# The chunk of the last 64 rows first, the weights' integer steps through a PSUM bank, the weights' conversions spread evenly

## The chip, the cores and the metric

The kernel runs on one core of a Trainium2 chip. A core has five engines that run side by side, each through its own list of instructions in order: PE (TensorE, matrix multiplies; its weight loads are shown as PEld), DVE (VectorE), ACT (ScalarE), POOL (GpSimd) and SP (SyncE, which here only issues DMA transfers). The metric is the device time of one execution in microseconds (us). Before the change it is 705.91 us, the median of three runs (705.66 to 707.59).

## The reference

An attention layer with a learned position bias feeds a two-matrix feed-forward layer. All arrays are float32.

```python
B, H, S, D = 4, 8, 576, 64            # batch, heads, rows, head width
scores = (1/sqrt(D)) * q @ k.T
rel = pos[:, None] - pos[None, :]
x = log1p(abs(rel)) / log1p(max(pos[:, None], 1))
bias = relu(x[..., None] @ w1 + b1) @ w2          # hidden 32, one column per head
attn = softmax(scores + bias per head)
x = (attn @ v) as 2304 rows of 512                # 2304 = B*S, 512 = H*D
h = relu(x @ w_in)                                # w_in 512 x 2048
out = (h*h) @ w_out                               # w_out 2048 x 512
```

## The kernel before

**Work by steps.** Batches are taken in pairs p = 0, 1. The 576 rows of a batch are cut into five chunks c: c = 1 to 4 are 128 rows each, and c = 0 is the last 64 rows. In a whole chunk the two batches of the pair lie side by side (nb = 2 blocks of 128 rows); in c = 0 the 64 rows of both batches share one block (nb = 1). A step is one (p, c, head): 10 chunks of 8 heads, 80 steps, counted here from 0. `ORDER` gives the order of the chunks, for pair 0 `[3, 0, 2, 4, 1]`. So steps 0 to 7 are chunk 3, steps 8 to 15 the half chunk 0, steps 16 to 23 chunk 2.

**A step.** `qk` writes the scores to PSUM (three fp16 products of split operands), `softmax_a` adds the bias and takes the maximum on DVE (line 367, one instruction for each block, with a small read of the maximum and the negation of line 370 behind it) and the exponential on ACT (line 373). `softmax_b` splits the result into two fp16 parts on ACT and POOL (lines 118, 384, 385), and a DMA transposes it. `pv` multiplies by v three steps later (`LAG`), and after a chunk's last head `finish_x` scales the chunk's rows, splits and transposes them.

**The bias.** The bias depends on the row and on the distance alone, so it is made once, in 36 groups of 16 rows, and written to a table in DRAM (`biasd`), from which each step reads its window (`bias_ld`, tile bt). `hgen` makes four hidden layers of a group (tile hg), each on DVE (line 266) or on ACT (line 263) as the digit of `HID` says (the digit is how many of the four go to ACT, one digit for two groups in their order of use); `bias_mm` multiplies them on PE (line 293), copies the result out on ACT or DVE (line 304) and stores it. A chunk's groups must be in DRAM before its first step; `bias_due` says how many groups are made by which step, `AHEAD` = 3 steps in advance.

**The weights.** w_in and w_out come in 32 loads of 512 KB (`WT`, called W below), through three staging buffers (stg) that k and v use too. Each is turned from float32, passed in as 64-bit words, into two fp16 parts. Three integer steps on DVE put the word's halves together (lines 185, 186, 188; tile cv in SBUF, which is input and output of the second and third), then ACT or POOL make the high part and POOL the low one (line 203). `W_AT` lists how many W are put behind k and v at each step.

**The feed-forward part.** A finished chunk becomes 8 units. A unit's `g1` is 24 matmuls into hp (line 465), then a ReLU on ACT, the square on DVE (line 473) and a split; `g2` (line 488) adds into one output bank for each block: o0, and for a whole chunk o1 as well. o0 and o1 have one PSUM bank each. A unit is started about once a step, and g2 runs three units behind g1 (`GLAG`). Units of a half chunk are half the width.

**The order.** The program is written step by step, and a scheduler of the tile framework then orders the instructions of each engine with its own estimates; the lists are fixed before the kernel runs.

Of the kernel before, what the change touches and what calls it, by code (L numbers as in the profile page):

```python
# [8 lines left out]
F32 = mybir.dt.float32  # L9
F16 = mybir.dt.float16  # L10
U32 = mybir.dt.uint32
# [5 lines left out]
B, H, S, D = 4, 8, 576, 64  # L17
# [15 lines left out]
    "ev": "AAAADD", "er": "AAAADA", "gh": "PPPPDD",  # L33
}

HID = "110033320111212000"

W_AT = [0, 0, 0, 0, 2, 0, 0, 0, 0, 2, 3, 0, 5, 0, 3, 4, 0, 4, 1, 0, 2, 1, 0, 2, 0, 0, 1, 0, 1, 0, 1, 0]
ORDER = [[3, 0, 2, 4, 1], [1, 0, 4, 2, 3]]
LAG, GLAG = 3, 3  # L40
BACKLOG = 10
AHEAD = 3
# [4 lines left out]
def tile_attention_moe(  # L47
# [11 lines left out]
    nc = tc.nc  # L59
    PS = bass.MemoryType.PSUM  # L60

    def pool(name, bufs, **kw):
        return ctx.enter_context(tc.tile_pool(name=name, bufs=bufs, **kw))
# [24 lines left out]
    ps_o = pool("ps_o", 1, space=PS)  # L88
# [75 lines left out]
    class WT:  # L164
# [14 lines left out]
        def split(self):  # L179
            u, q = self.u, self.part  # L180
            wd = self.st.bitcast(U32).rearrange("p (n t) -> p n t", t=2)
            lo32, hi32 = wd[:, :, 0], wd[:, :, 1]
            cv = r_p.tile([128, 512], F32, tag="r", name="cv")
            ci = cv.bitcast(U32)
            nc.vector.tensor_scalar(ci, hi32, 3, 0x3FFFFFFF, op0=ALU.logical_shift_left, op1=ALU.bitwise_and)  # L185
            nc.vector.scalar_tensor_tensor(out=ci, in0=lo32, scalar=29, in1=ci,  # L186
                                           op0=ALU.logical_shift_right, op1=ALU.bitwise_or)
            nc.vector.scalar_tensor_tensor(out=ci, in0=hi32, scalar=0xC0000000, in1=ci,  # L188
                                           op0=ALU.bitwise_and, op1=ALU.bitwise_or)
            if self.which == "i":  # L190
                st = cv.rearrange("p (k f) -> p k f", k=2)
                f0 = slice(u * 256, (u + 1) * 256)
                hi, lo, e = winH[:, 2 * q:2 * q + 2, f0], winL[:, 2 * q:2 * q + 2, f0], WIS
            else:
                st = cv
                hi, lo, e = woutH[:, u * 2 + q, :], woutL[:, u * 2 + q, :], WOS
            cast(zn("wh", u), hi, st, float(2 ** e))
            if zn("wl", u) == "D":
                nc.vector.scalar_tensor_tensor(
                    out=lo, in0=st, scalar=float(2 ** e), in1=hi, op0=ALU.mult, op1=ALU.subtract)  # L200
            else:
                cast(zn("wl", u), st, st, float(2 ** e))
                nc.gpsimd.tensor_tensor(lo, st, hi, op=ALU.subtract)  # L203
# [300 lines left out]

    order = [(p, c) for p in range(2) for c in ORDER[p]]
    steps = [(p, c, h) for p, c in order for h in range(H)]
    NS = len(steps)
    groups, due = [], []
# [2 lines left out]
        due.append(len(groups))  # L511

    def bias_due(t):
        k = (t + AHEAD) // H + 1
        if k >= NCK:
            return len(groups)
        f = (t + AHEAD) % H + 1
        return due[k - 1] + -(-(due[k] - due[k - 1]) * f // H)

    loads = deque()  # L520
# [5 lines left out]
    nls = []  # L526
    w_at = W_AT
    for h in range(H):
# [186 lines left out]
```

## Time and profile before

| what | value |
|---|---|
| median of three runs | 705.91 us |
| the profiled execution | 710.13 us |
| its span on the core | 708.4 us |
| PE busy | 611.1 us (86%) |
| DVE busy | 453.9 us (64%) |
| ACT busy | 357.3 us (50%) |
| POOL busy | 385.4 us (54%) |

The trace is of the profiled execution, so sums are made against its 710.13 us, of which 1.7 us lie outside the span. A profile row of an engine gives its busy share in 40 slices of the span; the shares over the whole span are averages over a first part and a second part that look quite different, so most rows below are of stretches of the span. "PEclk" is the granted clock of TensorE as a share of its full speed.

### The profile page before, as it was taken

How to read it: one execution, taken by the hardware profiler on the slowest of the kernel's cores; microseconds unless marked ns; L12 is line 12 of the kernel's file. 1: busy time of each engine (PE TensorE's matmuls, PEld its weight loads, DVE VectorE, ACT ScalarE, POOL GpSimd, SP SyncE). 2: the span in 40 equal slices, each digit the busy share in tenths (PEclk: the TensorE clock that was granted, in tenths of full speed). 3: DMA queues.
4: the chain of work that ended last, by engine and by line, in shares of the span. 5: the costliest groups of instructions: out<-in, count | busy, mean ns of one | idle time of the engine just before them, and what ended most of it. 6: DMA issues, size and time to landing. Idle time of an engine off the chain costs nothing.

```text
span 708.4 us, 15644 instructions
## 1 busy us (share of the span) xinstructions
PE 611.1 (86%) x6056; PEld 377.9 (53%) x6056; DVE 453.9 (64%) x977; ACT 357.3 (50%) x710; POOL 385.4 (54%) x375
## 2 busy tenths in 40 slices
PE   6635535687797998999998999999998999999997
PEld 1112213454454544666665667666665666676764
DVE  8687999699995687468757645335557656334120
ACT  5778645655676653654553453244464664531111
POOL 4266665568695544676676554435555566442211
PEclk9858557899797999999999999999999999999999
DMA  7699999997795898797896978375799978461000
GB/s 217 213 239 279 225 235 259 233 258 196 194 240 143 175 227 165 158 185 162 211 237 128 174 168 150 84 143 114 141 153 205 190 156 155 95 131 31 25 7 30
DMA packets 235881, 119.25 MB, mean 168 GB/s; under 512 B 196384, under 2 KB 212768, under 8 KB 235808
## 3 DMA queue, kind: packets, MB, share of 16 engines
q1 hardware_dynamic: 235808, 118.27, 74.1%
q8 instruction: 47, 0.77, 0.4%
q14 instruction: 26, 0.21, 0.1%
HBM read 55.44 MB, written 15.61 MB: 100 GB/s over the span
## 4 chain that ended last, share of the span: by engine, by line
PE 52%; DVE 18%; DMA 14%; issue 6%; ACT 5%; POOL 4%; SPq 0%; DVEq 0%; POOLq 0%; ACTq 0%
PE hp L465 20%; PE o L488 19%; DMA at<-a 7%; PE pv L411 5%; PE sc L352 3%; PE bp L293 3%; DVE hg L266 3%; DVE cv L186 3%; POOL a L385 2%; DVE s L367 2%; DVE cv L188 2%; DVE cv L185 2%; DMA biasd<-be 1%; ACT s L373 1%; ACT a L118 1%
## 5 line engine op out<-in xcount | busy, mean ns | idle before, releaser
L465 PE MATMUL hp<-xt,winH 128*128 128x256 f16 (+1 forms) x1280 | 202.4, 268 | 15.3 <-DVE r L473 14.0
L488 PE MATMUL o<-woutH,g 128*128 128x512 f16 x576 | 184.4, 380 | 0.9 <-ACT o L495 0.9
L373 ACT ACTIVATE s<-s,nm 128x576 f32<-128x576 f32 x144 | 110.5, 768 | 136.6 <-DVE nm L370 136.1
L465 PE MATMUL hp<-xt,winL 128*128 128x256 f16 (+1 forms) x640 | 165.7, 267 | 0.3 <-POOL winL L203 0.3
L385 POOL TENSOR_TENSOR a<-s,a 128x1024 f16<-128x1024 f32 (+1 forms) x80 | 162.6, 2033 | 0.0
L465 PEld LDWEIGHTS <-winH 128*128 128x128 f16 x1280 | 118.7, 100 | 51.3 <-issue 20.1
L367 DVE CUSTOM_DVE_ANT_0 s<-sc,bt 128x576 f32<-128x576 f32 x144 | 103.4, 750 | 45.3 <-PE sc L352 23.3
L488 PEld LDWEIGHTS <-g 128*128 128x128 f16 x864 | 82.8, 98 | 90.4 <-issue 6.7
L473 DVE TENSOR_TENSOR r<-hp,r 128x512 f32<-128x512 f32 (+1 forms) x80 | 50.6, 633 | 117.0 <-ACT r L471 116.6
L475 POOL TENSOR_TENSOR g<-r,g 128x512 f16<-128x512 f32 (+1 forms) x80 | 86.8, 1085 | 66.8 <-DVE g L122 64.4
L411 PEld LDWEIGHTS <-at 128*128 128x128 f16 (+1 forms) x2240 | 80.6, 105 | 71.3 <-DMA at<-a 38.7
L384 POOL TENSOR_TENSOR a<-s,a 128x128 f16<-128x128 f32 (+1 forms) x80 | 37.0, 463 | 146.5 <-ACT a L118 118.5
L411 PE MATMUL pv<-v,at 128*128 128x64 f16 (+1 forms) x2240 | 88.8, 199 | 30.7 <-DMA at<-a 28.9
L118 ACT ACTIVATE a<-s 128x1152 f16<-128x1152 f32 (+1 forms) x80 | 85.1, 1064 | 49.9 <-DMA at<-a 48.9
L488 PE MATMUL o<-woutL,g 128*128 128x512 f16 x288 | 109.4, 380 | 0.0
L471 ACT ACTIVATE r<-hp 128x512 f32<-128x512 f32 (+1 forms) x80 | 43.2, 540 | 64.9 <-PE hp L465 64.3
L266 DVE TENSOR_SCALAR hg<-tab_t,nb 128x352 f32<-128x352 f32 (+17 forms) x102 | 67.1, 708 | 13.1 <-PE bp L293 11.4
L293 PE MATMUL bp<-hg,w2s 128*32 128x288 f32 (+17 forms) x352 | 62.0, 550 | 14.8 <-ACT be L304 10.4
L465 PEld LDWEIGHTS <-winL 128*128 128x128 f16 x640 | 64.0, 100 | 8.2 <-issue 0.8
L352 PE MATMUL sc<-k,q 64*128 64x512 f16 x384 | 57.0, 398 | 0.0
L304 ACT ACTIVATE be<-bp,hcst 128x288 f32<-128x288 f32 (+32 forms) x80 | 34.5, 473 | 20.8 <-PE bp L293 14.4
L122 DVE TENSOR_SCALAR g<-r 128x512 f16<-128x512 f32 (+1 forms) x61 | 40.0, 656 | 2.1
(61 smaller groups left out, 551.4 us busy)
## 6 DMA issues: line engine op xcount, KB each, us to landing
bt<-biasd SPq DMA_DIRECT2D x64, 288.0 KB, 3.3
stg<-w_in SPq DMA_DIRECT2D x16, 512.0 KB, 4.3
stg<-w_out SPq DMA_DIRECT2D x16, 512.0 KB, 4.2
stg<-vd SPq DMA_DIRECT2D x16, 320.0 KB, 3.8
stg<-kd SPq DMA_DIRECT2D x16, 288.0 KB, 3.8
bt<-biasd SPq DMA_DIRECT2D x32, 144.0 KB, 3.5
qst<-qd SPq DMA_DIRECT2D x32, 128.0 KB, 3.5
out<-o SPq DMA_DIRECT2D x16, 256.0 KB, 2.4
```

The lines of the kernel that those rows point to most:

```text
L118: nc.scalar.activation(out=out, in_=in_, func=AF.Copy, scale=scale)
L266: nc.vector.tensor_scalar(ht, tab_t[:, 0:dlen(G)], scl[:, n:n + 1], nb1, op0=ALU.mult, op1=ALU.max)
L293: nc.tensor.matmul(out=bp[32 * t:32 * t + 32, 0:d1 - d0], lhsT=w2s, rhs=ts_[t][:, d0:d1], start=True, stop=True, tile_position=(0, 32 * t))
L352: nc.tensor.matmul(out=sc[:, 1024 * b:1024 * b + 512], lhsT=qt[r, qz, qs], rhs=kt[r, z, 64 * b:64 * b + 512], start=(n == 0), stop=(n == 2 ...
L367: nc.vector.tensor_tensor_reduce(s[:, 576 * b:576 * b + 576], sc[:, 960 * b:960 * b + 576], bt, inv, -3.0e38, ALU.add, ALU.max, mx[:, b:b ...
L373: nc.scalar.activation(out=sl, in_=sl, func=AF.Exp, bias=nm[:, b:b + 1], accum_out=su[:, h, b:b + 1])
L385: nc.gpsimd.tensor_tensor(av[:, :, 640:1152], ev[:, :, 0:512], av[:, :, 0:512], op=ALU.subtract)
L411: nc.tensor.matmul(out=dst, lhsT=lhsT, rhs=vt[:, vz, 5 * b + blk, :], start=(n == 0), stop=(n == 13), tile_position=(0, 0 if c else 64 * b))
L465: nc.tensor.matmul(out=hp[:, f * T:f * T + T].rearrange("p (b t) -> p b t", b=nb), lhsT=wt[:, k, c0:c0 + 128], rhs=xt[:, 0:nb, z * 4 + k, ...
L473: nc.vector.tensor_tensor(rr, hp[:, 0:2 * T], rr, op=ALU.mult)
L475: nc.gpsimd.tensor_tensor(g[:, 1, 0:2 * T], r[:, 0:2 * T], g[:, 0, 0:2 * T], op=ALU.subtract)
L488: nc.tensor.matmul(out=blk["o"][b], lhsT=g[:, z, c0:c0 + 128], rhs=wt[:, 2 * u + f, :], start=(u == 0 and f == 0 and z == 0 and wt is wout ...
```

## The change

Four things are changed together. The half chunk c = 0 of pair 0 becomes the first chunk (steps 0 to 7) and chunk 3 the second. The first two of the three integer steps of a W write to a tile `ci` in the PSUM bank of o1, and the third reads it from there and writes cv in SBUF. `W_AT` puts all 32 W into steps 0 to 15. `HID` is another table, and `bias_due` asks for the first chunk's groups alone before step 0 and looks ahead less in the first steps.

```diff
-HID = "110033320111212000"
+HID = "333222111111111000"
-W_AT = [0, 0, 0, 0, 2, 0, 0, 0, 0, 2, 3, 0, 5, 0, 3, 4, 0, 4, 1, 0, 2, 1, 0, 2, 0, 0, 1, 0, 1, 0, 1, 0]
-ORDER = [[3, 0, 2, 4, 1], [1, 0, 4, 2, 3]]
+W_AT = [1, 1, 2, 2, 2, 2, 2, 2, 3, 3, 3, 2, 2, 2, 2, 1] + [0] * 16
+ORDER = [[0, 3, 2, 4, 1], [1, 0, 4, 2, 3]]
...
             cv = r_p.tile([128, 512], F32, tag="r", name="cv")
-            ci = cv.bitcast(U32)
+            ci = ps_o.tile([128, 512], F32, tag="o1", name="ci").bitcast(U32)
             nc.vector.tensor_scalar(ci, hi32, 3, 0x3FFFFFFF, op0=ALU.logical_shift_left, op1=ALU.bitwise_and)
             nc.vector.scalar_tensor_tensor(out=ci, in0=lo32, scalar=29, in1=ci,
                                            op0=ALU.logical_shift_right, op1=ALU.bitwise_or)
-            nc.vector.scalar_tensor_tensor(out=ci, in0=hi32, scalar=0xC0000000, in1=ci,
+            nc.vector.scalar_tensor_tensor(out=cv.bitcast(U32), in0=hi32, scalar=0xC0000000, in1=ci,
                                            op0=ALU.bitwise_and, op1=ALU.bitwise_or)
...
     def bias_due(t):
-        k = (t + AHEAD) // H + 1
+        if t < 0:
+            return due[0]
+        ahead = min(AHEAD, t + 1)
+        k = (t + ahead) // H + 1
         if k >= NCK:
             return len(groups)
-        f = (t + AHEAD) % H + 1
+        f = (t + ahead) % H + 1
```

In the lists of the changed kernel the line numbers from 185 on are one higher. DVE just ahead of step 0 (the first line with ISA s,mx), before:

```order
L266 TENSOR_SCALAR hg<-tab_t,nb_131 128x528
L157 SCALAR_TENSOR_TENSOR v<-stg,v 128x640
L266 TENSOR_SCALAR hg<-tab_t,nb_131 128x544
L146 SCALAR_TENSOR_TENSOR k<-stg,k 128x576
L157 SCALAR_TENSOR_TENSOR v<-stg,v 128x640
L266 TENSOR_SCALAR hg<-tab_t,nb_131 128x560
L146 SCALAR_TENSOR_TENSOR k<-stg,k 128x576
L367 ISA s,mx<-sc,bt 128x576
```

The same place now:

```order
L189 SCALAR_TENSOR_TENSOR cv<-stg,ci 128x512
L157 SCALAR_TENSOR_TENSOR v<-stg,v 128x640
L186 TENSOR_SCALAR ci<-stg 128x512
L187 SCALAR_TENSOR_TENSOR ci<-stg,ci 128x512
L267 TENSOR_SCALAR hg<-tab_t,nb_131 128x304 x3
L189 SCALAR_TENSOR_TENSOR cv<-stg,ci 128x512
L267 TENSOR_SCALAR hg<-tab_t,nb_131 128x320 x2
L186 TENSOR_SCALAR ci<-stg 128x512
L187 SCALAR_TENSOR_TENSOR ci<-stg,ci 128x512
L368 ISA s,mx<-sc,bt 128x576
```

Ahead of step 0 stand 31 hg and no W before, and 10 hg and two whole W now. The second place is DVE ahead of step 16, the first of chunk 2 (r is the square of a feed-forward unit). Before:

```order
L186 SCALAR_TENSOR_TENSOR cv<-stg,cv 128x512
L188 SCALAR_TENSOR_TENSOR cv<-stg,cv 128x512
L266 TENSOR_SCALAR hg<-tab_t,nb_131 128x336
L473 TENSOR_TENSOR r<-hp,r 128x512
L266 TENSOR_SCALAR hg<-tab_t,nb_131 128x336 x2
L367 ISA s,mx<-sc,bt 128x576
```

And now (r is half as wide, and the hg are already those of chunk 4):

```order
L474 TENSOR_TENSOR r<-hp,r 128x256
L186 TENSOR_SCALAR ci<-stg 128x512
L187 SCALAR_TENSOR_TENSOR ci<-stg,ci 128x512
L189 SCALAR_TENSOR_TENSOR cv<-stg,ci 128x512
L186 TENSOR_SCALAR ci<-stg 128x512
L267 TENSOR_SCALAR hg<-tab_t,nb_131 128x416 x3
L187 SCALAR_TENSOR_TENSOR ci<-stg,ci 128x512
L424 TENSOR_TENSOR x<-pv,rd 128x256 x2
L368 ISA s,mx<-sc,bt 128x576
```

Of the 32 W, 11 stood behind step 16; now 2 do. Counted in the lists, this is what stands ahead of a step's first line 367 on DVE and first score matmul on PE (hp and o in matmuls):

| ahead of step | W | hg on DVE | r | bias matmuls | hp | o |
|---|---|---|---|---|---|---|
| 0, before / now | 0 / 2 | 31 / 10 | 0 / 0 | 11 / 8 | 0 / 0 | 0 / 0 |
| 8 | 7 / 12 | 38 / 30 | 0 / 0 | 76 / 76 | 0 / 0 | 0 / 0 |
| 16 | 21 / 30 | 58 / 48 | 3 / 2 | 100 / 88 | 72 / 24 | 24 / 0 |
| 24 | 32 / 32 | 76 / 69 | 10 / 10 | 132 / 128 | 240 / 216 | 96 / 48 |
| 32 | 32 / 32 | 102 / 96 | 19 / 19 | 176 / 176 | 456 / 456 | 144 / 144 |

The third place is ACT at the start of the program, where the hidden layers (hg), the copies of the bias (be) and k's corner (kz) stand. Before:

```order
L263 ACTIVATE hg<-tab_t,sm_t 128x320
L263 ACTIVATE hg<-tab_t,sm_t 128x304 x2
L263 ACTIVATE hg<-tab_t,sm_t 128x320
L304 ACTIVATE be<-bp,hcst 128x320
L304 ACTIVATE be<-bp,hcst 128x271
L151 ACTIVATE kz<-k 64x2x64 x2
L304 ACTIVATE be<-bp,hcst 128x304
```

And now:

```order
L264 ACTIVATE hg<-tab_t,sm_t 128x528 x3
L264 ACTIVATE hg<-tab_t,sm_t 128x544 x3
L264 ACTIVATE hg<-tab_t,sm_t 128x560 x3
L264 ACTIVATE hg<-tab_t,sm_t 128x576 x3
L151 ACTIVATE kz<-k 64x2x64 x2
L264 ACTIVATE hg<-tab_t,sm_t 128x320 x2
L305 ACTIVATE be<-bp,hcst 128x64
```

Twelve hidden layers of the half chunk's four groups now stand ahead of the first copy.

## Rows read from the trace of the kernel before

**Rows 1.** The page: the span, and the 40 slices of PE (tenths of a slice busy).

```profile
span 708.4 us, 15644 instructions
...
PE   6635535687797998999998999999998999999997
```

**Rows 2.** Where steps 0, 8, 16, 24 and 32 begin: the first line 367 of each in DVE's timeline (start us, us).

```profile
32.40 0.76 DVE L367 CUSTOM_DVE_ANT_0 s<-sc,bt 128x576 f32<-128x576 f32 x1
...
90.94 0.74 DVE L367 CUSTOM_DVE_ANT_0 s<-sc,bt 128x576 f32<-128x576 f32 x1
...
159.68 0.75 DVE L367 CUSTOM_DVE_ANT_0 s<-sc,bt 128x576 f32<-128x576 f32 x1
...
235.56 0.76 DVE L367 CUSTOM_DVE_ANT_0 s<-sc,bt 128x576 f32<-128x576 f32 x1 [1.45 <-DMA bt<-biasd]
...
301.07 0.76 DVE L367 CUSTOM_DVE_ANT_0 s<-sc,bt 128x576 f32<-128x576 f32 x1
```

**Rows 3.** The stretches between those steps: window, length, then busy us (instructions) of PE, PEld, DVE, ACT, POOL, granted clock, share of the DMA engines, GB/s.

```profile
32.00:91.00 59.00, 27.80 (x277) 12.61 (x277) 50.32 (x94) 43.56 (x87) 37.39 (x34) 0.67 0.95 252
91.00:160.00 69.00, 42.56 (x424) 25.51 (x424) 60.91 (x106) 38.68 (x78) 42.75 (x42) 0.78 1.01 245
160.00:236.00 76.00, 63.28 (x590) 34.82 (x588) 65.69 (x118) 47.74 (x94) 55.06 (x48) 0.87 0.80 192
236.00:301.00 65.00, 60.81 (x640) 33.41 (x637) 44.11 (x102) 36.35 (x77) 33.56 (x34) 1.00 0.85 183
301.00:361.00 60.00, 58.62 (x602) 39.42 (x600) 43.21 (x93) 32.45 (x70) 41.34 (x46) 1.00 0.85 191
```

**Rows 4.** The same for the instructions that touch cv alone; the first pair is DVE.

```profile
32.00:91.00 59.00, 21.16 (x23) 7.70 (x13) 7.79 (x6) 0.67 0.95 252
91.00:160.00 69.00, 31.87 (x43) 15.14 (x26) 20.78 (x18) 0.78 1.01 245
160.00:236.00 76.00, 33.45 (x31) 11.20 (x19) 19.83 (x16) 0.87 0.80 192
```

**Rows 5.** Shortest, median and longest duration in ns of the three integer steps and of the square, which reads PSUM.

```profile
L185 DVE TENSOR_SCALAR cv<-stg x32: 408/427/2353, 42.6 to 211.7; 128x512 uint32<-128x512 uint32 x32
...
L186 DVE SCALAR_TENSOR_TENSOR cv<-stg,cv x32: 654/750/2548, 43.3 to 214.1; 128x512 uint32<-128x512 uint32 x32
...
L188 DVE SCALAR_TENSOR_TENSOR cv<-stg,cv x32: 634/692/2619, 45.2 to 216.4; 128x512 uint32<-128x512 uint32 x32
...
L473 DVE TENSOR_TENSOR r<-hp,r x80: 407/691/693, 135.4 to 695.0; 128x512 f32<-128x512 f32 x64, 128x256 f32<-128x256 f32 x16
```

**Rows 6.** DVE and POOL side by side in two timelines (start us, us).

```profile
102.08 1.52 DVE L186 SCALAR_TENSOR_TENSOR cv<-stg,cv 128x512 uint32<-128x512 uint32 x1
...
101.73 1.33 POOL L385 TENSOR_TENSOR a<-s,a 128x512 f16<-128x512 f32 x1
```

**Rows 7.** Groups of DVE's instructions by shape: busy us, mean ns of one.

```profile
L367 DVE CUSTOM_DVE_ANT_0 s<-sc,bt 128x576 f32<-128x576 f32 x144 | 103.4, 750 | 45.3 <-PE sc L352 23.3 <-issue 7.1 <-PE sc L340 6.0
...
L370 DVE TENSOR_SCALAR nm<-mx 128x1 f32<-128x1 f32 x144 | 18.8, 146 | 0.2
L449 DVE SCALAR_TENSOR_TENSOR xh<-x,cc,xh 128x512 f16<-128x512 f32 x18 | 17.6, 995 | 0.1
...
L448 DVE TENSOR_SCALAR xh<-x,cc 128x512 f16<-128x512 f32 x18 | 9.9, 585 | 0.2
...
L266 DVE TENSOR_SCALAR hg<-tab_t,nb 128x384 f32<-128x384 f32 x8 | 5.4, 740 | 1.5 <-ACT s L373 1.5
...
L266 DVE TENSOR_SCALAR hg<-tab_t,nb 128x320 f32<-128x320 f32 x6 | 2.7, 505 | 0.0
```

**Rows 8.** A wait of DVE between 32 and 160 us: total us, times, longest.

```profile
DVE s L367 <- POOL a L385: 3.7, 2, 1.9
```

**Rows 9.** Pieces of the chain that ended last (start us, us): the way to step 0, and feed-forward work of whole and half chunks.

```profile
24.51 4.14 DMA biasd<-be
...
28.74 3.63 DMA bt<-biasd
...
528.18 1.29 PE o L488 x6
...
639.61 2.62 PE hp L465 x24
```

**Rows 10.** A half chunk's hp and the bias matmuls, in the same chain and in the groups by line.

```profile
526.73 1.45 PE hp L465 x24
...
L293 PE MATMUL bp<-hg,w2s 128*32 128x288 f32 (+17 forms) x352 | 62.0, 550 | 14.8 <-ACT be L304 10.4 <-ACT hg L263 2.9 <-DVE hg L266 0.8
```

**Rows 11.** ACT at the start: the first hg (timeline: start, us), and one hg and one be by shape (busy us, mean ns).

```profile
4.51 2.26 ACT L263 ACTIVATE hg<-tab_t,sm_t 128x320 f32<-128x320 f32 x4 [2.29 <-DVE tab_t L607]
...
L263 ACT ACTIVATE hg<-tab_t,sm_t 128x544 f32<-128x544 f32 x3 | 2.4, 833 | 0.0
...
L304 ACT ACTIVATE be<-bp,hcst 128x272 f32<-128x272 f32 x3 | 1.5, 486 | 0.1
```

**Rows 12.** A whole chunk's bias window among the DMA issues (KB each, us to landing), and two shorter stretches in the columns of rows 3.

```profile
bt<-biasd SPq DMA_DIRECT2D x64, 288.0 KB, 3.3
...
55.00:70.00 15.00, 8.28 (x74) 2.83 (x70) 10.52 (x24) 13.22 (x29) 9.37 (x9) 0.94 1.06 287
...
115.00:120.00 5.00, 4.69 (x67) 3.27 (x68) 5.00 (x17) 2.62 (x7) 1.61 (x3) 0.66 1.13 344
```

## The prediction

> **What bounds the kernel now.** I read the page first: PE is busy over 90% of nearly every slice of the second half, but only half busy in the first quarter [rows 1]. So the end is set by PE's total work, plus what PE loses at the start, and only the start can be changed by this edit. Then I looked for a point from which both programs have the same work ahead. The counts in the section on the change give it: ahead of step 32 both have made all 32 W, the same 456 hp and 144 o matmuls, 19 squares and all bias groups, and from there the lists are alike. Before, step 32 begins at 301.1 us [rows 2], and from there PE is busy 58.6 of 60 us, 97.7% [rows 3]. So the question is one: when does step 32 begin now?
>
> Next I read the stretches between steps 0, 8, 16, 24 and 32. Between 32 and 160 us DVE is busy 50.3 of 59 and 60.9 of 69 us, while PE does 27.8 and 42.6 us, at a granted clock of 0.67 and 0.78 (so largely at the lower of its two levels, 1.2 GHz) [rows 3]. DVE bounds that part. From 160 us on PE is busy 63.3 of 76 and 60.8 of 65 us, so it bounds more and more there. The three integer steps of the W cost DVE 21.2, 31.9 and 33.5 us in the first three stretches [rows 4]: 86.5 us for 32 W, 2.70 us each. Yet their shortest durations are 0.41, 0.65 and 0.63 us, 1.70 in all, and their longest over 2.3 us [rows 5]. The timelines show why: a second step that started at 102.08 took 1.52 us, until 103.60, while POOL ran a subtraction until 103.06; about 0.54 us of it lie behind POOL's end [rows 6]. A DVE instruction that takes two tensors from SBUF is held while POOL is at work.
>
> **The change part by part, first the price of a W.** Now the second and third steps read one tensor from SBUF and one from PSUM, and no trace shows that form. The nearest row is the square, which reads PSUM, has 512 elements like them, and shows a median of 0.691 and a longest of 0.693 us: nothing holds it [rows 5]. From below stand their own shortest, 0.65 and 0.63. The first step writes to PSUM; from below it is 0.41 and from above 0.69. I take 0.65 for each, the shortest of the like-shaped second step, so 1.95 us for a W. The ends are 1.70 (all at their shortest, a gain) and 2.70 (nothing is won; excluded only if POOL's hold is what I read it to be).
>
> The Trainium skill, in "VectorE: DVE Perf Modes", section "Why PSUM operands drop a tier", speaks against part of this: a float32 instruction with any operand in PSUM runs at one element per cycle, so the first step loses the faster mode that its 0.41 us [rows 5] suggests. By that rule it costs what the second does, which is the sum below; without it the first step stays at 0.41, and with 28 W between steps 0 and 16 step 16 comes 28 x 0.24 = 6.7 us earlier (694.2 us at the end).
>
> **Until step 0.** ACT is the way there: the first hg starts at 4.51 us [rows 11]. Now 12 hg at 0.83 (10.0 us) and 12 be at no more than 0.49 (5.9) stand ahead of the last store, with three hg at 2.26 / 4 = 0.57 (1.7) and six kz and two weight casts between, which I estimate at 2.5 us from their small shapes: 24.6 us. Before, the store on the chain starts at 24.51, the load of the bias at 28.74, the step at 32.4 [rows 2, 9]. No change; 31 to 35 us as bounds, as two more stores now stand ahead of the load on SP. Two W are done by then.
>
> **Steps 0 to 7, the half chunk.** Of DVE's 50.3 us, 50.3 - 21.2 = 29.1 are not W. One block instead of two saves 8 x (0.75 + 0.146) = 7.2 us [rows 7]. The new HID and the later bias put 20 hg here instead of 7: 13 x 0.62 (the middle of 0.505 and 0.740, the shapes of these groups [rows 7]) = 8.1 us more. 10 W cost 19.5. Sum 29.1 - 7.2 + 8.1 + 19.5 = 49.5. DVE idled 8.7 us here; 3.7 of it were waits for POOL to free a step's buffer [rows 8], which half steps need less; 5.0 remain. Step 8 at 32.4 + 54.5 = 86.9 us (90.9 before).
>
> **Steps 8 to 15, now a whole chunk.** 60.9 - 31.9 = 29.0, plus 7.2 for the second block, less 2 hg (1.2), less one of two xh pairs of the half chunk that finishes here (0.995 + 0.585 = 1.6 [rows 7]), plus 18 W (35.1): 68.5, and the 8.1 us of idle time as before. Step 16 at 86.9 + 76.6 = 163.5 us (159.7 before). So the crowded weights cost 3.8 us up to here.
>
> **Steps 16 to 31.** DVE is left with 2 W, and 65.7 - 33.5 + 3.9 + 44.1 = 80 us of work: it no longer bounds. PE does. It had 63.3 + 60.8 = 124.1 us here [rows 3]. It is further behind at step 16: before, 72 hp and 24 o matmuls were done, 3 x 2.62 + 4 x 1.29 = 13.0 us; now 24 half-width hp, 1.45 us [rows 9, 10]: 11.6 us more to do. 12 bias matmuls more at 62.0 / 352 = 0.176 us are 2.1 us [rows 10]. Sum 137.8 us. Of the old 63.3 us about (1 - 0.87) x 63.3 = 8.2 were lost to the clock; the granted clock was 1.00 wherever PE had over 90% [rows 3], which it now has, so I take 129.6 us, and at 97.7% busy 132.6 (141.0 if no clock comes back). Step 32 at 163.5 + 132.6 = 296.1 us, against 301.1: 5.0 us earlier.
>
> **The sum.** The profiled execution took 710.13 us; 705.1 is what it would take. It lies 4.2 us above the median of 705.91, so from the median: 700.9 us.
>
> Hidden: HID moves six hg from DVE to ACT, which is busy 43.6 of 59 us at most [rows 3]. The bank of o1 is a wait only if a W still comes when a whole chunk's g2 begins; the last W stands between steps 16 and 24, the first 48 o of the half chunk end there too, so W never queue behind an output.
>
> **Rivals.** *No change.* The half chunk first leaves PE 11.6 us behind, and only half of the clock's loss returns: 133.7 / 0.977 = 136.8 us, step 32 at 300.3, 705.1 us. For it: PE's granted clock at step 16 follows a sparse stretch; against: from 236 us on it never fell.
>
> *Slower: the DMA engines become the bound in steps 8 to 15.* They are at a share of 1.01 there already, at 245 GB/s: 16.9 MB [rows 3]. Added are 4 W (2.1 MB), 8 bias windows at 288 instead of 144 KB (1.2 MB [rows 12]) and 8 transposes of 18 blocks of 128 x 128 fp16 instead of 9 (2.4 MB): 22.6 MB. At 245 GB/s that is 92.2 us instead of 76.6, and all is 15.6 us later: 716.5 us. It decides below 22.6 MB / 76.6 us = 295 GB/s. Against it: 287 GB/s were moved over 15 us (78.7 us, 703.0 at the end) and 344 over 5 us [rows 12].
>
> *A larger gain.* W at 1.70 us (7.1 us) and half of DVE's remaining 13.1 us idle gone (6.5), since fewer instructions are held: step 32 at 282.5, 687.3 us. Against it: the rest of DVE's two-tensor instructions are held as before.
>
> **How the numbers follow.** Forecast 0.42, no change 0.20, slower 0.25, larger gain 0.13. The forecast's own bounds are 693.8 (W at 1.70) to 709.3 (no clock back). A measurement of this kernel tells about 0.3%, 2.1 us, from no change: 703.8 to 708.0. Faster: 0.13, and 0.38 of the forecast: 0.51. Same: most of the second case and some of the forecast and of the slower one: 0.20. Slower: 0.29, with W that stay at 2.70 us (28 x 0.75 = 21 us, 721.9) at its far end. For 8 in 10 the range is 684 to 717 us.
>
> **What will show it.** Right: the three steps at about 0.65 us with hardly a longer one; step 16 within 5 us of 163.5; PE over 95% busy at a clock of 1.00 from there; step 32 near 296. Wrong: integer steps still over 1.5 us beside POOL; DVE waiting for stg between steps 8 and 16 (the slower rival); PE idle between steps 16 and 32, which would mean that steps wait for their transposes rather than for PE, and that work left behind costs more than its own length.

## The result and the profile after

The changed kernel took 714.73 us (median of four runs, 713.15 to 715.45) against 705.79 us for the kernel before on the same chip: a ratio of 1.0118, 95% interval 1.0093 to 1.0142. It is slower by 1.2%; 0.7% faster was forecast. The two profiled executions differ less, 713.15 against 710.13 us, because that of before lay 4.2 us above its median and that of after 1.6 us below. So what the traces show is 3 of the 9 us, and the rest of this section reads them stage by stage.

The page of after, first its span and PE's 40 slices, which answer to [rows 1]:

```profile
span 711.0 us, 15677 instructions
...
PE   4655446456689999999998999999998999999997
```

PE is emptier than before in the first twelve slices, and fuller behind them. The starts of steps 0, 8, 16, 24 and 32 (first line 368 of each in DVE's timeline; start us, us; a bracket gives idle time before and what ended it) answer to [rows 2]:

```profile
36.55 0.76 DVE L368 CUSTOM_DVE_ANT_0 s<-sc,bt 128x576 f32<-128x576 f32 x1 [0.78 <-DMA bt<-biasd]
...
99.56 0.73 DVE L368 CUSTOM_DVE_ANT_0 s<-sc,bt 128x576 f32<-128x576 f32 x1
...
178.23 0.74 DVE L368 CUSTOM_DVE_ANT_0 s<-sc,bt 128x576 f32<-128x576 f32 x1
...
233.88 0.76 DVE L368 CUSTOM_DVE_ANT_0 s<-sc,bt 128x576 f32<-128x576 f32 x1 [4.11 <-DMA bt<-biasd]
...
304.52 0.76 DVE L368 CUSTOM_DVE_ANT_0 s<-sc,bt 128x576 f32<-128x576 f32 x1 [0.33 <-PE sc L353]
```

Step 16 begins 18.5 us later than before, step 32 only 3.4 us later. From step 32 to the end of the span it is 406.5 us, before 407.3: the two lists really are alike from there. The stretches between those steps, in the columns of [rows 3]:

```profile
36.60:99.60 63.00, 34.74 (x300) 15.93 (x300) 52.38 (x90) 38.89 (x81) 35.87 (x45) 0.61 0.94 248
99.60:178.20 78.60, 44.92 (x486) 26.44 (x486) 66.50 (x137) 51.58 (x100) 47.55 (x44) 0.64 1.05 262
178.20:233.90 55.70, 46.32 (x523) 26.61 (x523) 41.91 (x98) 37.79 (x77) 36.68 (x37) 0.97 0.84 185
233.90:304.50 70.60, 70.54 (x634) 39.26 (x632) 45.88 (x102) 35.00 (x72) 34.51 (x33) 1.00 0.66 151
304.50:364.50 60.00, 59.79 (x612) 40.35 (x611) 42.06 (x94) 33.11 (x71) 41.58 (x46) 1.00 0.89 198
```

Up to step 16 DVE is busy 118.9 of 141.6 us, and the DMA engines have a share of 0.94 and 1.05 at the same time; PE runs at a granted clock of 0.61 and 0.64, near its lower level of 1.2 GHz. From step 16 on PE is busy 116.9 of 126.3 us at a clock of 0.97 and 1.00. The integer steps themselves, by the view of one tile (min/median/max ns), answer to [rows 5]:

```profile
L186 DVE TENSOR_SCALAR ci<-stg x32: 667/690/695, 12.5 to 181.8; 128x512 uint32<-128x512 uint32 x32
L187 DVE SCALAR_TENSOR_TENSOR ci<-stg,ci x32: 682/696/706, 13.2 to 183.8; 128x512 uint32<-128x512 uint32 x32
L189 DVE SCALAR_TENSOR_TENSOR cv<-stg,ci x32: 669/686/689, 24.8 to 186.1; 128x512 uint32<-128x512 uint32 x32
```

None is held any more: the longest of all 96 is 0.706 us, where before single ones took over 2.3. A W costs DVE 2.07 us, the sum of the three medians, instead of 2.70. So the edit does on DVE what it says, and the kernel is slower all the same.

### The profile page after: what moved, and what is told of

It is laid out like the page before. It is cut to its first block, busy times and chain, and to the rows that moved or that the text cites. A ratio compares the mean times of both kernels' runs of the same rounds, so it can differ in the third digit from the quotient of the medians.

```text
span 711.0 us, 15677 instructions
## 1 busy us (share of the span) xinstructions
PE 612.6 (86%) x6056; PEld 380.0 (53%) x6056; DVE 433.4 (61%) x971; ACT 359.8 (51%) x716; POOL 371.7 (52%) x375
## 4 chain that ended last, share of the span: by engine, by line
PE 52%; DMA 18%; DVE 11%; POOL 6%; ACT 6%; issue 5%; SPq 1%; DVEq 0%; POOLq 0%; ACTq 0%
PE hp L466 19%; PE o L489 19%; DMA at<-a 11%; PE pv L412 6%; PE sc L353 3%; PE bp L294 3%; DMA biasd<-be 2%; DVE s L368 2%; DVE hg L267 2%; POOL a L386 2%; DMA stg<-kd 2%; ACT a L118 2%; ACT s L374 1%; DMA bt<-biasd 1%; PE sc L341 1%
## 5 line engine op out<-in xcount | busy, mean ns | idle before, releaser
L374 ACT ACTIVATE s<-s,nm 128x576 f32<-128x576 f32 x144 | 110.4, 767 | 146.1 <-DVE nm L371 136.0
L386 POOL TENSOR_TENSOR a<-s,a 128x1024 f16<-128x1024 f32 (+1 forms) x80 | 159.6, 1994 | 0.1
L412 PEld LDWEIGHTS <-at 128*128 128x128 f16 (+1 forms) x2240 | 83.1, 108 | 72.7 <-DMA at<-a 42.3
L385 POOL TENSOR_TENSOR a<-s,a 128x128 f16<-128x128 f32 (+1 forms) x80 | 34.8, 435 | 163.1 <-ACT a L118 142.9
L412 PE MATMUL pv<-v,at 128*128 128x64 f16 (+1 forms) x2240 | 90.4, 203 | 32.3 <-DMA at<-a 32.3
L294 PE MATMUL bp<-hg,w2s 128*32 128x288 f32 (+17 forms) x352 | 60.5, 616 | 16.2 <-ACT be L305 11.1
L267 DVE TENSOR_SCALAR hg<-tab_t,nb 128x464 f32<-128x464 f32 (+17 forms) x96 | 64.7, 722 | 11.8 <-PE bp L294 8.7
L264 ACT ACTIVATE hg<-tab_t,sm_t 128x320 f32<-128x320 f32 (+17 forms) x48 | 33.5, 735 | 12.5 <-PE bp L294 10.2
L122 DVE TENSOR_SCALAR g<-r 128x512 f16<-128x512 f32 (+1 forms) x61 | 38.3, 627 | 2.1
## 6 DMA issues: line engine op xcount, KB each, us to landing
qst<-qd SPq DMA_DIRECT2D x32, 128.0 KB, 3.2
```

Of the source, the lines that this page charges most:

```text
L267: nc.vector.tensor_scalar(ht, tab_t[:, 0:dlen(G)], scl[:, n:n + 1], nb1, op0=ALU.mult, op1=ALU.max)
L294: nc.tensor.matmul(out=bp[32 * t:32 * t + 32, 0:d1 - d0], lhsT=w2s, rhs=ts_[t][:, d0:d1], start=True, stop=True, tile_position=(0, 32 * t))
L374: nc.scalar.activation(out=sl, in_=sl, func=AF.Exp, bias=nm[:, b:b + 1], accum_out=su[:, h, b:b + 1])
L386: nc.gpsimd.tensor_tensor(av[:, :, 640:1152], ev[:, :, 0:512], av[:, :, 0:512], op=ALU.subtract)
L412: nc.tensor.matmul(out=dst, lhsT=lhsT, rhs=vt[:, vz, 5 * b + blk, :], start=(n == 0), stop=(n == 13), tile_position=(0, 0 if c else 64 * b))
```

## The experiments

Times of the kernel before scattered between 704 and 717 us on the chips used, so each run is compared by its ratio to the kernel before on its own chip. W in steps 0 to 15 counts the first integer steps in DVE's timeline between the starts of steps 0 and 16; the stage lengths come from the same timelines, and DVE's idle time is the length of steps 0 to 15 less DVE's busy time in them.

| kernel | order, spread | ratio (95%) | W in steps 0-15 | steps 0-15, us | of it DVE idle, us | steps 16-31, us | step 32 at, us |
|---|---|---|---|---|---|---|---|
| before | old, old | 1 | 22 | 127.3 | 16.7 | 141.4 | 301.1 |
| after | new, new | 1.0118 (1.0093-1.0142) | 28 | 141.7 | 22.7 | 126.3 | 304.5 |
| e1 steps in SBUF | new, new | 1.0212 (1.0178-1.0245) | 30 | 152.0 | 6.2 | 124.7 | 314.3 |
| e2 PSUM alone | old, old | 0.9947 (0.9920-0.9974) | 20 | 122.7 | 28.6 | 142.0 | 296.8 |
| e3 | new, old | 1.0318 (1.0291-1.0345) | 16 | 105.8 | 21.4 | 174.1 | 318.7 |
| e4 other bank | new, new | 1.0134 (1.0089-1.0180) | 29 | 146.1 | 24.2 | 126.0 | 309.8 |
| e5 | old, new | 1.0205 (1.0159-1.0250) | 29 | 149.2 | 36.8 | 121.8 | 317.3 |
| e6 start HID | new, new | 1.0092 (1.0057-1.0128) | 29 | 150.0 | 27.1 | 128.0 | 308.1 |
| e7 | new, middle | 1.0139 (1.0097-1.0181) | 22 | 122.3 | 18.2 | 152.4 | 311.7 |
| e8 old bias times | new, new | 1.0060 (1.0039-1.0081) | 29 | 149.7 | 25.4 | 117.8 | 307.4 |
| e9 half the bytes | new, new | 0.9913 (0.9885-0.9942) | 27 | 127.8 | 10.9 | 127.4 | 290.9 |
| e10 one integer step | new, new | 0.9871 (0.9840-0.9903) | 30 | 129.5 | 43.0 | 124.8 | 289.1 |
| e11 | old, later | 1.0113 (1.0078-1.0148) | 17 | 123.4 | 33.9 | 152.5 | 308.1 |
| e12 before, half the bytes | old, old | 0.9962 (0.9940-0.9985) | 22 | 125.3 | 11.7 | 139.1 | 296.7 |
| e13 both cheap | new, new | 0.9659 (0.9583-0.9735) | 30 | 126.0 | 35.5 | 120.4 | 280.5 |
| e14 no POOL part | new, new | 0.9968 (0.9934-1.0003) | 28 | 138.7 | 29.3 | 124.9 | 300.9 |
| e15 low parts on DVE | old, old | 1.0025 (1.0001-1.0048) | 20 | 121.7 | 26.8 | 148.5 | 302.5 |
| e16 before, both cheap | old, old | 0.9565 (0.9501-0.9628) | 24 | 124.3 | 43.7 | 115.7 | 271.7 |
| e17 two steps | old, old | 0.9841 (0.9809-0.9874) | 20 | 116.5 | 33.7 | 139.9 | 288.4 |
| e18 two steps | new, new | 0.9865 (0.9842-0.9888) | 29 | 129.9 | 24.5 | 123.8 | 289.9 |

The scheduler orders the lists anew for every kernel, so no run changes one thing alone: with the new W_AT 27 to 30 W fall into steps 0 to 15, and e4, which only takes another bank than after, has those steps 4.4 us longer. The stage lengths are of one profiled execution each, so a difference of some 5 us between two of them tells little by itself.

**The PSUM bank by itself: e1, e2 and e4.** The theory after reading the traces was that the bank wins and the crowded weights lose more; the rivals were that the bank wins nothing, and that the half chunk first is what costs.

e1, in the changed kernel:

```diff
-ci = ps_o.tile([128, 512], F32, tag="o1", name="ci").bitcast(U32)
+ci = cv.bitcast(U32)
```

> The changed kernel, but the weights' first two integer steps write the SBUF tile cv again; order of the chunks, HID and W_AT stay new. Theory (the PSUM bank wins, the crowded weights lose): about 0.65 us per W more on DVE, 20 us in all, of which the first 16 steps can hide a part behind transfers: 720 to 733 us. Rival A (the PSUM bank is worth nothing, because DVE does not bound that part): 713 to 717 us, as the changed kernel.

e2, in the kernel before (e4 has the same line in the changed kernel instead of o1):

```diff
-ci = cv.bitcast(U32)
+ci = ps_h.tile([128, 512], F32, tag="h", name="ci").bitcast(U32)
...
-nc.vector.scalar_tensor_tensor(out=ci, in0=hi32, ...
+nc.vector.scalar_tensor_tensor(out=cv.bitcast(U32), in0=hi32, ...
```

> The kernel before, but the integer steps leave their results in a PSUM bank (one of the two of hp and bp, since the bank of the second output is in use while W still come in the old order); nothing else is changed. Theory: DVE, which bounds the steps 0 to 15 there, has 20 us less to do, and 3 to 9 us of it reach the end: 697 to 703 us. Rival A: 704 to 708 us, as before.

> The changed kernel with the integer steps in a bank of hp and bp instead of the bank of the second output, so that the other runs that use this bank can be compared with it. All theories: 713 to 717 us, as the changed kernel; if it is over 718, the shared bank makes hp and bp wait, and the others have to be read with that.

Without the bank the new order is 0.9% slower (e1 against after); with it alone the old order is 0.5% faster, 704.67 us against 708.02. By its time e2 lies in the range of rival A (704 to 708 us) and above that of the theory, since the kernel before was slower on this chip; but its interval is clear of 1, and that of e1 clear of that of after, so rival A falls, though e2's gain of 3.4 us is at the low end of what was expected. The other bank costs nothing that the totals can tell (e4 against after, overlapping intervals), but it is not free: in steps 0 to 15 of e4 PE's bias matmuls wait 13.4 us for the third integer step to release it (us in total, times, longest):

```profile
PE bp L294 <- DVE cv L189: 13.4, 6, 5.0
```

So the runs that use this bank carry such a wait where W come close together. What else is changed (order, spread, HID and bias times) costs 1.9%, e4 against e2, or 1.7%, after against e2. **e2 is faster than both kernels and computes the same.**

**Spread and order apart: e3, e5, e7 and e11.** Each is a line of W_AT, and the order where the table says so.

```diff
 e3: -W_AT = [1, 1, 2, 2, 2, 2, 2, 2, 3, 3, 3, 2, 2, 2, 2, 1] + [0] * 16
     +W_AT = [0, 0, 0, 0, 2, 0, 0, 0, 0, 2, 3, 0, 5, 0, 3, 4, 0, 4, 1, 0, 2, 1, 0, 2, 0, 0, 1, 0, 1, 0, 1, 0]
 e7: +W_AT = [0, 0, 1, 1, 1, 1, 1, 1, 2, 2, 2, 2, 2, 2, 2, 2, 2, 2, 1, 1, 1, 1, 1, 1] + [0] * 8
 e11 (in e2): +W_AT = [0, 0, 0, 0, 2, 0, 0, 0, 0, 0, 0, 2, 3, 0, 5, 0, 3, 4, 0, 4, 1, 0, 2, 1, 0, 2, 0, 0, 1, 0, 1, 1]
```

> The changed kernel with the old W_AT (W from step 4 to 30, most between 9 and 17) and the integer steps in a bank of hp and bp; the half chunk still goes first. Theory (the crowded weights make step 0, steps 4 to 7 and step 16 late): step 0 back at 32 to 33 us, step 16 below 170 us, 697 to 704 us. Rival B (the half chunk first is what costs, because PE is left 11.6 us behind): 712 us or more.

> The kernel before with the integer steps in a bank of hp and bp (as in e2) and with the new W_AT; the whole chunk 3 still goes first, HID and the bias times are the old ones. Theory now (weights made before step 16 lie on the path, since PE has nothing else to do there; made later they lie beside PE's work): step 16 comes 10 us or more later than in e2 (154.7), and the end is 710 to 720 us. Rival B (the half chunk first is what costs): no later than e2, 698 to 706 us.

> The changed kernel with one W in each of steps 2 to 7, two in 8 to 17 and one in 18 to 23 (24 steps instead of 16), integer steps in a bank of hp and bp. Theory (each W ahead of step 16 costs its time, and one after it is hidden if it still comes before its square): about 10 W fewer ahead of step 16, which comes at 155 to 165 us (183.8 in e4); the end at 703 to 711 us. Rival B (half chunk first): 712 us or more whatever the spread. Between them: if W after step 16 hold back g1, steps 24 to 32 get longer, as in e3, where step 32 came at 318.7.

> e2 (old order, integer steps in a bank of hp and bp) with the W from step 9 on made one or two steps later, so that 15 instead of 19 are made ahead of step 16. Theory (bytes ahead of step 16 cost 512 KB at 0.25 MB per us, 2 us each): step 16 8 us earlier than in e2, at 147 us; at the end 698 to 704 us if PE catches up, as in e2 or later (704 to 712) if PE then waits for weights, as it does in e3.

The first half of the theory holds in e3, e5 and e7: step 16 comes as early as the W ahead of it are few. In the new order 16, 22 and 29 W make stages of 105.8, 122.3 and 146.1 us, (146.1 - 105.8) / 13 = 3.1 us per W (2.7 between the first two, 3.4 between the last two, and 3.0 with after's 28 W and 141.7 us in the place of e4); in the old order 20 and 29 W make 122.7 and 149.2, 2.9 us per W. e11 with 17 does not lie on that line: it was to bring step 16 8 us earlier than in e2 and brought it 0.9 us later, so at 123.4 us something else bounds. The second half falls: an early step 16 is not an early end. Two windows of 40 us in the columns of [rows 3], of e3 and of after:

```profile
200.00:240.00 40.00, 24.98 (x173) 10.98 (x174) 27.38 (x54) 18.18 (x34) 14.28 (x18) 0.54 0.71 193
```

```profile
200.00:240.00 40.00, 36.13 (x398) 20.01 (x395) 24.51 (x58) 26.69 (x55) 21.70 (x21) 1.00 0.88 199
```

In e3 PE is not filled where after fills it. The last W begins at 262.6 us there, and hp and o stand in the program behind the W that they read, so I take late W for the reason that e3, e7 and e11 ended late (e5 ended above its range too, though step 16 came late as expected). The waits do not show it. In steps 16 to 31 of e3 PE waited 21.3 us for transposes and about 4 us for parts of weights, and of the 47.8 us that these steps are longer than in after, 15.4 are PE's own busy time, at a lower clock (132.3 us at 0.81, 116.9 at 0.99). The bank of hp and bp has its part too: in steps 16 to 31 PE waits 8.1 us in e7, 4.2 in e11, 3.6 in e3 and 3.6 in e2 for DVE to release it.

Rival B named 712 us or more for e3 and e7, and both lie there. It does not hold alone, for e5 and e11 in the old order are slow too. But it does not fall either: with the old spread, the new order (with its HID and bias times) is 3.7% slower than the old one (e3 against e2). With the new spread the old order is the slower one by 0.7%, and there the intervals overlap a little (e5 against e4). So the order and the spread have to be read together: early weights cost steps 0 to 15, late ones cost steps 16 to 31.

**The start and the bias times: e6 and e8.**

```diff
 e6: -HID = "333222111111111000"
     +HID = "113222111111111000"
 e8: the old bias_due in place of the new one
```

> The changed kernel with HID 11 instead of 33 for the first four groups, so that DVE makes 12 of their 16 hg and ACT 4. Theory of the start (12 hg, the kz copies and 8 be all stand on ACT, and step 0 waits for ACT's last be): step 0 at 31 to 34 us instead of 36.6, and 2 to 4 us at the end: 710 to 713. Rival C (step 0 waits for the third load of k, whose kz stands ahead of be on ACT, whoever makes hg): step 0 at 36 to 38 us, 713 to 717 us.

> The changed kernel with the old function bias_due, which makes seven groups ahead of step 0 instead of four, and keeps three steps ahead from there. Theory: step 0 later by 3 groups at 2 to 3 us on ACT, at 42 to 46 us; steps 0 to 4 shorter by less than that: 714 to 720 us. Rival D (the bias that is made late is what holds steps 4 to 8 and step 16): step 8 and step 16 as early as before or earlier, below 710 us.

In e6 step 0 does begin early, at 30.07 us, so the theory of the start was right and rival C wrong; yet step 4 begins at 62.74, 1.9 us later than in after. Two rows of DVE's timeline, of e6:

```profile
30.07 0.74 DVE L368 CUSTOM_DVE_ANT_0 s<-sc,bt 128x576 f32<-128x576 f32 x1
...
62.74 0.75 DVE L368 CUSTOM_DVE_ANT_0 s<-sc,bt 128x576 f32<-128x576 f32 x1
```

The 6.5 us are lost within four steps, and the end cannot be told from that of after (overlapping intervals). DVE has 3.0 us more work in these four steps (23.5 against 20.4 us), since two hg, a v and a part of a W more stand in them; another 5.4 us are idle time. In e8 step 0 came at 40.0 and step 16 at 189.6 us, among the latest of all, and still its ratio is 0.6% below that of after, with the interval below too. Neither the theory (714 to 720) nor rival D (an earlier step 8) fits. Its trace does not show the gain: steps 16 to 31 take only 117.8 us, but step 32 begins 2.9 us later than in after, and the profiled execution is longer (714.37 against 713.15 us, on another chip). So the new bias times may be some of what the change costs; that is not settled.

**What a crowded W costs, and where: e9, e10, e12, e14, e13 and e16.** Now the question was whether DVE or the DMA engines bound steps 0 to 15.

```diff
 e9, e12: -src = w_in[q * 256:(q + 1) * 256, u * 256:(u + 1) * 256].rearrange("(k p) f -> p k f", p=128)
          +src = w_in[q * 256:q * 256 + 128, u * 256:(u + 1) * 256]
 ...
          +lo32, hi32 = (wd[:, 0:256, z].rearrange("p (a n) -> p a n", a=1).to_broadcast([128, 2, 256]) for z in (0, 1))
 e10:     the scalar_tensor_tensor steps at 187 and 189 left out, ci = cv
 e14:     -cast(zn("wl", u), st, st, float(2 ** e))
          -nc.gpsimd.tensor_tensor(lo, st, hi, op=ALU.subtract)
          +cast(zn("wl", u), lo, st, float(2 ** e))
 e13, e16: e9 and e10 together, in the changed kernel and in the one before
```

> The changed kernel, but each W loads 256 instead of 512 KB and computes on the loaded half twice: the instructions of DVE, ACT and POOL keep their number and size, the other half of each W is left out of the result. Theory (the DMA engines bound steps 0 to 15; about 28 W there, 7.3 MB at 0.25 MB per us are 29 us): step 16 at 150 to 165 us instead of 178, until DVE's 119 us of work and its idle time bound; 695 to 707 us. Rival F (DVE's work, or waits that do not depend on the bytes, bound): step 16 at 174 to 180, 712 to 716 us.

> The changed kernel with only the first of the three integer steps, written into cv; the low bits and the sign of the weights are left out. DVE has some 1.6 us less per W, 46 us before step 16; the bytes stay. Theory (DMA engines): step 16 at 168 to 178 us, and 705 to 714 us at the end. Rival F (DVE bounds): step 16 at 140 to 155 us, below 700 us.

> The kernel before with the same halving of each W's load as in e9 (19 W ahead of step 16, 5 MB; the other half of each W is left out of the result). Theory (its steps 0 to 15 are bound by the DMA engines too, with DVE close behind): step 16 at 148 to 156 us instead of 159.7; 696 to 703 us. Rival G (DVE alone bounds it there, as the prediction read it): step 16 at 158 to 161, 704 to 708 us.

> The changed kernel without GpSimd's subtraction for the low part of each W; ACT writes its scaled cast straight into winL and woutL, so the low parts are not the reference's. POOL has 32 x 1.2 us less, 34 of it ahead of step 16; DVE and the bytes stay. Theory (the transposes wait on SP behind POOL's queue, and each W lengthens it): step 16 at 162 to 172 us, 701 to 709 at the end. Rival (POOL is off the way): step 16 at 175 to 180, 712 to 716 us.

> The changed kernel with both: half of each W's bytes and one integer step (the same parts left out as in e9 and e10). If a W's price is a chain (load, then DVE, then the casts): the two gains of 14 us add up, step 16 at 148 to 153 us, 684 to 690 at the end. If they only make room for a third bound: step 16 at 158 to 165, 694 to 699 us.

> The kernel before with both halvings of e13 (the same parts left out), in the old order and spread. If the half chunk first and the new spread gain by themselves once a W is cheap: 5 us or more above e13. If the new order costs by itself: at or below e13.

Steps 0 to 15 in the columns of [rows 3], of e9:

```profile
35.60:163.40 127.80, 75.99 (x767) 38.90 (x768) 116.94 (x229) 89.38 (x179) 83.35 (x88) 0.67 0.93 221
```

of e10:

```profile
34.80:164.30 129.50, 72.75 (x729) 36.12 (x729) 86.49 (x174) 90.12 (x184) 88.19 (x91) 0.70 1.04 267
```

and of e13:

```profile
34.10:160.10 126.00, 75.66 (x754) 39.96 (x755) 90.50 (x176) 91.13 (x187) 89.49 (x93) 0.66 0.91 228
```

In e9 DVE does its work as in after, 116.9 against 118.9 us, but idles 10.9 us instead of 22.7: with half the bytes of the weights in flight, half of DVE's idle time is gone, and 2.05% of the total. Step 16 and the end lie in the ranges of the DMA theory. Yet DVE's own waits for a W's load are 3.6 us in both; what is gone is a wait for PE's pv (5.3 us in after) and parts of others, so the bytes cost mostly by way of other engines. In e10 it is the other way round: DVE has 32 us less to do, the DMA engines stay at 1.04, and 2.5% are won. The end lies in rival F's range; step 16, at 164.3 us, in neither (168 to 178, 140 to 155). DVE now idles 43.0 us, and 18.6 of them are waits for loads:

```profile
DVE cv L186 <- DMA stg<-w_out: 12.6, 5, 4.8
DVE cv L186 <- DMA stg<-w_in: 6.0, 5, 2.0
```

So neither theory is right alone; either resource, relieved, lets the stage shrink by 12 to 14 us. In e9 DVE then holds it, busy 116.9 of 127.8 us; in e10 the loads do in part. e18 below comes to 129.9 us, nearly the same, with 13.5 us of DVE's work taken away instead of 32, so what e10 takes beyond that buys nothing there. Both together (e13) give step 16 only some 4 us more, as its second case said (158 to 165 us), so a third bound waits at about 126 us, with DVE at 90.5 and the DMA engines at 0.91; which one it is stays open. Its end, 685.08 us, fits the first case (684 to 690): at step 32 e13 is 8.6 us ahead of e10, half of it behind step 16. In the old order halving the bytes won only 0.4% (e12), with step 16 at 157.7 us, between the two theories, and the end, 705.0 us, in rival G's range. That the loads matter less there because 14 instead of 18 W stand in steps 8 to 15 is likely, but not shown.

e14 made an unlooked-for point. Its 225 DVE instructions of steps 0 to 15 are those of after, in another order, and yet they are 9.5 us shorter (109.4 against 118.9), as these groups by line of after

```profile
L267 DVE TENSOR_SCALAR hg<-tab_t,nb 128x416 f32<-128x416 f32 (+7 forms) x38 | 23.7, 666 | 1.9 <-PE bp L294 1.9
...
L157 DVE SCALAR_TENSOR_TENSOR v<-stg,v 128x640 f16<-128x640 f32 x5 | 7.4, 1472 | 3.8 <-POOL v L120 3.8
```

and of e14 show (busy us, mean ns, idle time before them):

```profile
L266 DVE TENSOR_SCALAR hg<-tab_t,nb 128x416 f32<-128x416 f32 (+7 forms) x38 | 18.4, 535 | 3.6 <-PE bp L293 3.6
...
L157 DVE SCALAR_TENSOR_TENSOR v<-stg,v 128x640 f16<-128x640 f32 x5 | 4.1, 825 | 4.7 <-POOL v L120 3.3 <-ACT v L118 1.4
```

POOL has 32 subtractions less (28 of them in steps 0 to 15), and DVE's hg and v are no longer held by them. Step 16 came only 2.2 us earlier, against an expected 6 to 16, and lies in the rival's range: DVE idled the more, 29.3 us. At the end 1.5% were won, 706.65 us, within the theory's 701 to 709. So POOL's part of a W costs something, but that the transposes behind POOL's queue bound steps 0 to 15 is not supported.

**Order against price: e15, e17 and e18.**

```diff
 e15 (in e2): -"wl": "AAAAAAAP"
              +"wl": "ADADADAP"
 e17 (in e2), e18 (in the changed kernel):
-nc.vector.scalar_tensor_tensor(out=ci, in0=lo32, scalar=29, in1=ci,
-                               op0=ALU.logical_shift_right, op1=ALU.bitwise_or)
```

> e2 (old order, integer steps in a bank of hp and bp) with the low parts of every second W made by DVE in one instruction instead of by ACT and POOL: DVE 14 x 0.7 to 1.0 us more, POOL 14 x 1.25 and ACT 14 x 0.62 less. Theory (POOL holds the transposes, and DVE has room since e2): 698 to 703 us. Rival (DVE is the tighter of the two): 705 to 712 us.

> e2 without the second integer step: the lowest three bits of each weight's mantissa are left out. DVE has 0.69 us less per W, 14 us ahead of step 16; bytes, casts and order stay. If DVE's part of a W is on the way in the old order as in e10 (17 us for 1.6 us per W): 7 us below e2, 696 to 700 us. If the old order is bound elsewhere: 702 to 706 us.

> The changed kernel without the second integer step (the same bits left out as in e17). By e10, 7 us below the changed kernel: 706 to 709 us. If the gap between the orders is the price of crowded weights alone, it shrinks in step with that price: from 13 us (e4 against e2) to 8 to 11 us above e17. If the order costs by itself whatever a W costs: still 12 to 14 us above e17.

e15 is 0.8% slower than e2: steps 0 to 15 are 1.0 us shorter, but steps 16 to 31 are 6.4 us longer; giving POOL's work to DVE does not pay, as the rival said, and e2 stays the best that computes the same. e17 wins 1.1% over e2 (8.4 us at step 32 for 32 x 0.69 = 22 us less on DVE), as expected. e18 wins 2.5% over after, 14.6 us at step 32, where 1% was expected. With that, the gap between the orders shrinks from 1.7% (after and e2, the same banks as here) to 0.2%, within the intervals. With weights cheap in both ways it is 0.9% with overlapping intervals (e13 and e16), never in the new order's favour; by its medians, 6.1 us below e13, e16 fell where the new order was to cost by itself. So the half chunk first, together with the new spread, costs nothing that can be told once a W is 0.69 us cheaper on DVE. That the 1.7% are the price of W at full cost, crowded ahead of step 16, fits this and e5; it is not shown for all of them, since HID and the bias times are part of the gap as well. I had expected the gap to shrink in step with the price; it is gone after a third of it, and why is open.

## Why the prediction was wrong, by its own steps

*The price of a W, 1.95 us:* 2.07 measured, with no hold at all. The mechanism was right, the size 0.12 us short (3.4 us on 28 W); the first step did lose its 0.41 us, as the rule of the Trainium skill has it ("VectorE: DVE Perf Modes", section "Why PSUM operands drop a tier"), and the trace agrees: median 0.690 us into PSUM, 0.427 into SBUF before [rows 5]. DVE's busy time fell from 453.9 to 433.4 us, 20.5 us, with six hg fewer on DVE among them.

*Step 0 at 32.4 us, no change:* 36.6. Wrong, by a term left out: ACT's be stand in one row with kz, and kz waits for a load and DVE. ACT's timeline of after (in brackets idle time and what ended it):

```profile
21.11 0.63 ACT L151 ACTIVATE kz<-k 64x128 f16<-64x128 f16 x2 [3.25 <-DVE k L146]
21.76 1.04 ACT L305 ACTIVATE be<-bp,hcst 128x256 f32<-128x256 f32 x3
24.42 0.49 ACT L305 ACTIVATE be<-bp,hcst 128x272 f32<-128x272 f32 x1 [1.62 <-DMA biasd<-be]
25.55 0.63 ACT L118 ACTIVATE winH<-cv 128x512 f16<-128x512 f32 x1 [0.64 <-DVE cv L189]
```

The 24.6 us of work were summed as if ACT never waited; 3.25 + 1.62 + 0.64 = 5.5 us of waits stand among these rows, the first behind the third load of k, the others behind a buffer that be and cv share and behind a W. But e6, with step 0 6.5 us earlier, ends no earlier, so these us were hardly on the way to the end.

*Steps 0 to 15:* DVE's work was forecast at 49.5 + 68.5 = 118.0 us and was 118.9, with some luck: the two parts were 52.4 and 66.5, and their errors nearly cancel. The **idle time** was forecast at 5.0 + 8.1 = 13.1 us, carried over from before less one wait, and was 10.6 + 12.1 = 22.7. With step 0's 4.2 us that is all of step 16's delay, 178.2 instead of 163.5. This is the step that failed: idle time was taken to be a constant of the stage, and weights to cost DVE's instructions alone. The runs put the price of a W ahead of step 16 at 2.7 to 3.4 us instead of 1.95, and e9 shows that half of the idle time goes with half of the weights' bytes.

The step fails even where the order and the spread stay the old ones. Steps 0 to 15 of the kernel before and of e2, in the columns of [rows 3]:

```profile
32.40:159.70 127.30, 70.06 (x698) 37.86 (x698) 110.61 (x197) 81.89 (x163) 79.83 (x76) 0.73 0.98 249
```

```profile
32.00:154.70 122.70, 70.34 (x708) 35.71 (x708) 94.11 (x186) 77.75 (x155) 69.71 (x74) 0.73 1.01 245
```

In e2 the bank takes 16.5 us of work from DVE, the stage gets 4.6 us shorter, and the other 11.9 us turn into idle time, 28.6 instead of 16.7. In e1, the changed kernel with the integer steps in SBUF, DVE has 26.9 us more to do than in after, the stage is 10.3 us longer, and the idle time is 6.2 us. So DVE did not bound these steps in the sense of the prediction, by which what it saves shortens them one for one.

Waits of DVE and of PE in after, from the views of waits (us in total, times, longest), first DVE in steps 0 to 15, then PE in steps 8 to 15:

```profile
DVE x L424 <- PE pv L412: 5.3, 3, 2.6
DVE v L157 <- POOL v L120: 3.8, 3, 1.8
DVE ci L186 <- DMA stg<-w_in: 2.6, 2, 2.4
```

```profile
PE pv L412 <- DMA at<-a: 21.4, 7, 4.6
```

DVE's largest wait is for PE's pv, and pv waits 21.4 us for transposes. Nine of them are issued in these steps, with a median of 6.4 us from issue to landing:

```profile
at<-a SPq DMA_TRANSPOSE x9, 6.4
```

In e9 the median is 5.5, but PE waits for them for 21.9 us still, so this wait alone does not explain the stage. Nor is it new: steps 8 to 15 hold the whole chunk in after and the half chunk before, and over steps 0 to 15 the wait grew only from 20.3 us before to 24.9 in after, as these rows of the two views show.

```profile
PE pv L411 <- DMA at<-a: 20.3, 8, 5.5
```

```profile
PE pv L412 <- DMA at<-a: 24.9, 9, 4.6
```

What makes up the rest of the idle time stays open.

*Steps 16 to 31:* forecast 132.6 us, measured 126.3. The clock came back as said (0.97 and 1.00 against 0.87 in [rows 3]), and PE was less far behind: when step 16 began on DVE it had made 96 half-width hp and 12 o matmuls rather than the 24 and none of the forecast, which had counted what the list puts ahead of the step's score matmul (counted as now, it was 86 and 24 before). PE's work was 116.9 us, not 129.6, at 92.6% busy instead of 97.7. This error partly cancels that of steps 0 to 15, by luck: step 32 at 304.5 us, 8.4 us after the forecast, where step 16 was 14.7 us after it.

*The rest:* 8.1 us of the 13.8 between 700.9 and 714.73 are in the profiled executions, 705.1 and 713.15. The other 5.8 come from setting the forecast 4.2 us below the profile, where after's profile lay 1.6 below its median.

*The rivals:* the slower one, DMA engines that bound in steps 8 to 15, named 716.5 us, near the measured 714.73 by luck: it had the resource, but not the place. It set 295 GB/s as the rate below which it decides, and 262 were moved; its 22.6 MB were 262 GB/s x 78.6 us = 20.6 MB, and the stage took 78.6 us, near the forecast's 76.6 and not the rival's 92.2. Its sign, DVE waiting for stg in steps 8 to 15, came to 3.3 us. The loss lay in steps 0 to 7, 63.0 instead of 54.5 us, where I had not looked at the loads though their share was 0.95 before [rows 3]. And e10 and e18 say that DVE's work was as much on the way as the loads were. "No change" and "a larger gain" fall.

*Hidden:* the bank of o1 is no wait, as said: no row of DVE's waits in steps 0 to 15 has it, and the other bank is no faster (e4).

## What to carry to other kernels

Where one engine is busy 84% and the DMA engines have a share of 1 in the same stage, work brought into that stage costs more than its time on the engine: a W of 2.07 us on DVE made the stage 3 us longer. And work taken out of it gives back less than its time: of 16.5 us less on DVE, e2 kept 4.6. Forecast the idle time of such a stage anew, with the loads that come in; the term summed from durations alone was right to 1% (118.0 and 118.9 us) and the stage still 10 us short. Time each separable part of a change by itself: the PSUM bank alone (e2) was better than the whole.

## What was not expected of the hardware

A float32 tensor_scalar of DVE with one tensor in SBUF, hg, is held beside POOL as well as those with two: 666 ns on average in after, 535 without POOL's 32 subtractions, on the same 38 instructions of steps 0 to 15. The Trainium skill has it so ("SBUF — State Buffer", section "Who interferes with whom": a tensor_scalar can enter a mode that takes the pair of ports shared with GpSimd), and the trace agrees; the prediction had told of two-tensor instructions only, though the first integer step, with one tensor, took up to 2.353 us before [rows 5]. With a PSUM destination it is not held: 667 to 695 ns on all 32, whatever POOL did.

An earlier start can be worth nothing: 6.5 us won at step 0 (e6) were gone at step 4, for the four steps took 8.4 us longer, 3.0 of them DVE's work and 5.4 its idle time.
